# A spectral gated mix on one Trainium2 core: PSUM written in runs of 32 in place of every second place, and the last stores from two queues

## The chip, the cores and the metric

The kernel runs on one core of one Trainium2 chip. The metric is device time in microseconds, the median over runs of the whole program. Before the change it is 128.46 us (three runs, 128.43 to 128.71).

## The reference

Both branches are given the same x; a second x among the inputs is not used. What is computed, cut to what matters:

```python
# x: (1, 2048, 1024) bf16; w_r, w_i: (2048, 513) each, for A and for B; gate_w: (1024)
def branch(x, w_r, w_i):
    X = rfft2(x.astype(float32), axes=(-2, -1))
    return irfft2(X * (w_r + 1j * w_i), s=(2048, 1024)).astype(bfloat16)

g = sigmoid((x * gate_w).sum(-1, keepdims=True))     # one number a row
out = g * branch(x, A_w_r, A_w_i) + (1 - g) * branch(x, B_w_r, B_w_i)
```

So there is one forward transform of x, two products with weights, and two backward transforms that are mixed row by row.

## The kernel before, in words

The transforms are done as matmuls with constant matrices that are loaded from HBM. A helper, `Prog`, records every operation with what it reads and writes; each engine then runs its own operations in the order in which they were recorded, with semaphore waits only where another engine's result or buffer is needed. An engine never goes past an operation that waits, and neither does the queue of DMA issues of an engine (SP's and POOL's here; ACT issues one load at the very start).

In order of time:

- Stage 1 (`stage1`, L380): x is loaded, folded on DVE (L345), and multiplied on PE with the first factor of the transform over the 2048 rows. The results go to the tile FT on ACT (L389) and DVE (L387).
- Steps 0 to 15 (`step`): `stage4(i)`, `swap(i)`, `stage2(i + 2)`, and `products`. `stage2` does the transform over the 1024 columns. For odd columns it issues 8 matmuls of 128 columns (L443), for even ones 8 matmuls of 64 columns (L452); together they fill two banks of PSUM, eight blocks of 128 columns. ACT copies these 1024 columns to XF as bf16 (L458); it reads them in the order in which the next stage wants them. The banks are 0 and 1 for all steps but `stage2(1)` (4 and 5) and `stage2` of 9, 11, 13 and 15 (6 and 7). `stage4(i)` does the rest of the transform over the rows, 4 wide matmuls (L473) on the copy, and ACT evicts them (L477). `swap(i)` issues two DMAs that exchange partitions (from POOL's queue in steps 0 to 7, from SP's later). DVE multiplies the result and its exchanged twin by the weights (`product`, L490), in an order written out by hand (`ORDER`). Weights are loaded through SP's queue until about 48 us. In steps 0 to 5, PE also computes the spectrum of the gate (`gate_spectrum`, L502), two times 8 small matmuls a step.
- The first factor of the backward transform over the rows (`group`, L594): 32 groups of 16 matmuls, evicted by ACT (L604) and DVE (L602). Groups 0 to 15 need the first half of the products, 16 to 31 the second. Small pieces of work lie between them (`zsum` L541, `col0` L568, `rbgen` L581).
- Stages 6 and 7, for each of 16 row blocks r: `stage6` (L725) does the second factor and mixes the branches with the gate, and ACT evicts (L735); `stage7` (L750) does the backward transform over the columns. ACT copies one half (L757); DVE forms sums and differences (L797) and POOL the last ones (L802). In blocks 5, 8 and 12 (`HALF`) and in 14 and 15 DVE does the last ones itself (L761). Then the block is stored, 256 KB, from SP's queue (L290 is the line of every DMA issue); block 15 in two stores of 128 KB each.

SP waits for all stores at the end (L835).

The order of the 256 columns within a block of constants for the odd columns, `F2`, and the places in PSUM of odd and even columns:

```python
F2 += [F[0], F[1]]                                              # odd columns
o = ps((b0 + t % 2) * 512 + cs * 256 + 64, [(64, 2), (1, 64)])             # L443: two runs of 64
o = ps((b0 + t % 2) * 512 + cs * 256 + v, [(193 - 2 * v, 2), (2, 32)])     # L452: two times 32 places, 2 apart
dst, src = sl(XF, CSo(i), [(1, 1024)]), ps(b0 * 512, [(128, 8), (1, 64), (64, 2)])   # L458
```

The pairs in an access pattern are (step, count), the outermost first. A place of PSUM is one float32.

Of the kernel before, what the change touches and what calls it, by code (L numbers as in the profile page):

```python
# [25 lines left out]
def make_consts():  # L26
# [27 lines left out]
    F2 = []  # L54
    for cmb, par in ((0, 0), (1, 1), (2, 1), (3, 0)):
        l = 2 * (np.r_[0:64, 128:192, 64:128, 192:256] if par else np.r_[0:64, 129:193, 64:128, 193:256, 128])[None, :] + par
        th = pi2 * l * (dd + 0.5) / 1024
        F = (np.cos(th) if cmb < 2 else np.sin(th)).reshape(2, 128, 256)
        if par:
            F2 += [F[0], F[1]]  # L60
        else:
            F = F[0].reshape(128, 2, 2, 32, 2)
            e = [np.stack([F[:, :, 0, :, w], F[:, :, 1, :, 1 - w]], axis=2).reshape(128, 128) for w in range(2)]
            F2 += e if cmb == 0 else e[::-1]
# [45 lines left out]
    l2, sl_, f = row % 2, (row // 2) % 32, row // 64  # L110
# [15 lines left out]
    for pi in range(2):  # L126
        for h in range(2):
# [5 lines left out]
            a = pi2 * l * (d + 0.5) / 1024  # L133
# [101 lines left out]
def bass_gated_mix__spectral_gfnet__spectral_gfnet__prompt_kernel(nc, A_x, A_w_r, A_w_i, B_x, B_w_r, B_w_i, gate_w, out):  # L235
# [29 lines left out]
    def sl(t, off, dims, p0=0, np_=128, pstep=1):  # L265
        n = t.shape[1]
        return AP(t, p0 * n + off, [[n * pstep, np_]] + [list(x) for x in dims])

    def ps(col, dims):
        return AP(PS, col, [[4096, 128]] + [list(x) for x in dims])  # L270
# [18 lines left out]
    def dma(eng, name, dst, src, **kw):  # L289
        return P.add(eng, lambda e: e.dma_start(dst, src), dma=name, **kw)  # L290
# [143 lines left out]
    def stage2(i, css=(0, 1), ab=(0, 1)):  # L434
        hf, p = divmod(i, 8)
        b0 = 4 if i == 1 else 6 if i in (9, 11, 13, 15) else 0
        if 0 in ab:
            for cs in css:
                for t in (2 * p, 2 * p + 1):
                    for j in range(2):  # L440
                        o = ps((b0 + t % 2) * 512 + cs * 256 + 64, [(64, 2), (1, 64)])
                        rh = sl(F2, 256 + 512 * cs + 256 * j + hf * 128, [(1, 128)])
                        P.add("pe", lambda e, o=o, cs=cs, j=j, t=t, rh=rh: e.matmul(o, fblock(1 + cs, j, t), rh, start=(j == 0), stop=(j == 1)),  # L443
                              r=[("F1", cs, j), "F2"], w=[bank(b0 + t % 2)])
        if 1 in ab:
            for cs in css:
                for t in (2 * p, 2 * p + 1):
                    for w in range(2):
                        v = 1 - w if cs else w
                        o = ps((b0 + t % 2) * 512 + cs * 256 + v, [(193 - 2 * v, 2), (2, 32)])  # L450
                        rh = sl(F2, 1280 * cs + w * 128 + hf * 64, [(1, 64)])
                        op = P.add("pe", lambda e, o=o, cs=cs, t=t, w=w, rh=rh: e.matmul(o, fblock(3 * cs, w, t), rh, start=True, stop=True),  # L452
                                   r=ekeys(p, cs, w) + ["F2"], w=[bank(b0 + t % 2)])
        if css == (0,) or ab == (0,):
            return
        dst, src = sl(XF, CSo(i), [(1, 1024)]), ps(b0 * 512, [(128, 8), (1, 64), (64, 2)])
        kw = dict(r=[bank(b0), bank(b0 + 1)], w=[("CS", i % 3)], after=last1)
        P.add("act", lambda e: e.activation(dst, src, ACT.Copy), **kw)  # L458
        return op
# [280 lines left out]
    def stage7(r):  # L740
        nonlocal pqc
        full, half = r >= 14, r in HALF
        b0 = 2 * (r - 14) if r >= 14 else 4 + 2 * (r % 2)
        oo = OUo + (r % NOU) * 1024
        es = sl(WA, EOo + (r % 2) * 1024, [(1, 1024)]).bitcast(f32)

        def mm(col, c0, n, ri, pi, h, k, last):
            lh = sl(WA, Yo + (pi * 4 + ri * 2 + h) * 2048 + r * 128, [(1, 128)])
            rh = sl(FT, DIo + pi * 2048 + (ri * 2 + h) * 256 + c0 * 4096, [(4096, n), (1, 256)])
            P.add("pe", lambda e: e.matmul(ps(col, [(1, n * 256)]), lh, rh, start=(k == 0), stop=(k == last)),  # L750
                  r=[("Y", r), "DI"] + ["DJ"] * (full or half), w=[bank(col // 512)])

        def ods(s, k, n):
            return sl(WA, oo + 1023 * s + 512 * (1 - 2 * s) * k, [(512 * (1 - 2 * s), n), (1 - 2 * s, 256)])

        def even(c0, n):
            P.add("act", lambda e: e.activation(es[:, :n], ps((b0 + 1) * 512 + c0, [(1, n)]), ACT.Copy), r=[bank(b0 + 1)], w=[("EO", r % 2)], after=[last5])  # L757

        def finals(k0, n, bk, t, o, keys):
            for s, op in enumerate((ALU.add, ALU.subtract)):  # L760
                P.add("dve", lambda e, s=s, op=op: e.tensor_tensor(  # L761
                    out=ods(s, k0, n), in0=ps(bk * 512, [(256, n), (1, 256)]),
                    in1=sl(t, o + 512 * k0, [(1, 512 * n)]).bitcast(f32).rearrange("p (a b) -> p a b", a=n), op=op),
                    r=keys + [bank(bk)], w=[("OU", r % NOU, s, k) for k in range(k0, k0 + n)], after=[last5])

        if full:
            for k in range(4):
                mm((b0 + 1) * 512, 0, 2, 1, k // 2, k % 2, k, 3)
            even(0, 512)
            for k0, n, bk in ((0, 2, b0),) if r == 14 else ((0, 1, b0), (1, 1, 4)):  # L770
                for k in range(4):
                    mm(bk * 512, k0, n, 0, k // 2, k % 2, k, 3)
                finals(k0, n, bk, WA, EOo + (r % 2) * 1024, [("EO", r % 2)])
        elif half:
            for e_ in range(2):
                for k in range(2):
                    mm((b0 + 1) * 512 + e_ * 256, 0, 1, 1, k, k ^ e_, k, 1)
            even(256, 256)
            for k in range(4):
                mm(b0 * 512, 0, 2, 0, k // 2, k % 2, k, 3)  # L780
            to = 4096 + (r % 2) * 1024
            for s, op in enumerate((ALU.add, ALU.subtract)):
                P.add("dve", lambda e, s=s, op=op: e.tensor_tensor(out=sl(MM, to + s * 512, [(1, 512)]).bitcast(f32),
                                                                   in0=ps((b0 + 1) * 512, [(1, 256)]), in1=es[:, :256], op=op),
                      r=[("EO", r % 2), bank(b0 + 1)], w=[("T", r % 2, s), ("GM", 1, 0), ("GM", 1, 1)])
            finals(0, 2, b0, MM, to, [("T", r % 2, 0), ("T", r % 2, 1)])
        else:
            for e_ in range(2):
                for ri in range(2):
                    for k in range(2):  # L790
                        mm((b0 + e_) * 512 + ri * 256, 0, 1, ri, k, k ^ e_, k, 1)
            even(0, 512)
            pk = pqc % NPQ
            pqc += 1
            pq = PQo + pk * 2048
            for s, op in enumerate((ALU.add, ALU.subtract)):
                P.add("dve", lambda e, s=s, op=op: e.tensor_tensor(out=sl(WA, pq + s * 1024, [(1, 1024)]).bitcast(f32), in0=ps(b0 * 512, [(1, 512)]),  # L797
                                                                   in1=es, op=op),
                      r=[("EO", r % 2), bank(b0)], w=[("PQ", pk, s)], after=[last5])
            pv = sl(WA, pq, [(1, 2048)]).bitcast(f32).rearrange("p (a b c) -> p a b c", a=2, b=2)  # L800
            for s, op in enumerate((ALU.add, ALU.subtract)):
                P.add("pool", lambda e, s=s, op=op: e.tensor_tensor(out=ods(s, 0, 2), in0=pv[:, :, 0, :], in1=pv[:, :, 1, :], op=op),  # L802
                      r=[("PQ", pk, 0), ("PQ", pk, 1)], w=[("OU", r % NOU, s, k) for k in range(2)])
        ou = lambda ks: [("OU", r % NOU, s, k) for s in range(2) for k in ks]
        if r < 15:
            return [dma("sp", f"o{r}", outv[:, r, :], sl(WA, oo, [(1, 1024)]), r=ou((0, 1)))]
        both = lambda a: a.rearrange("p (a b) -> p a b", b=256)[:, ::3, :]
        return [dma("sp", "o15a", both(outv[:, r, :]), sl(WA, oo, [(768, 2), (1, 256)]), r=ou((0,))),
                dma("sp", "o15b", outv[:, r, 256:768], sl(WA, oo + 256, [(1, 512)]), r=ou((1,)))]

    outs = []
    stage6(0)
    stage6(1)
    for r in range(16):
        if 0 < r < 14:
            stage6(r + 2)
        outs += stage7(r)
        if r == 0:
            stage6(2)

    with nc.Block() as block:
        sems = {}
# [59 lines left out]
```

## Time and profile before

| | us |
|---|---|
| median of three runs | 128.46 |
| the profiled execution | 128.5 |
| its span, first to last instruction | 126.7 |
| outside the span | 1.8 |

| engine | busy us | share of the span |
|---|---|---|
| DVE | 101.6 | 80% |
| ACT | 98.8 | 78% |
| POOL | 43.0 | 34% |

The granted TensorE clock is 0.99 of full speed. In 40 slices of 3.2 us each, the rows of PE and of the DMA engines are (9 is 90% or more):

```
PE   0398899799999999999999999999799999999930
DMA  3999999999999995336995000000000332444247
```

The DMA engines are full until about 48 us with loads at some 360 GB/s, and are then used in part: for exchanges, for the last constants until about 70 us, and for stores from 97 us on. A group's row in the profile reads: line, engine, operation, written and read tiles, shapes, count, busy time, mean ns of one, and idle time before. A matmul's duration is its way through the array; the distance of two starts is what a matmul costs in a row of them.

### The profile page before, as it was taken

The page shows a single profiled execution, that of the slowest core. Times are in us where ns is not written, and L with a number is a line of the kernel's source. Part 1 is how long each engine was busy: PE and PEld are TensorE (multiplying, and loading weights), DVE is VectorE, ACT ScalarE, POOL GpSimd, SP SyncE. Part 2 cuts the span into 40 slices and gives each one's busy share as a digit, 9 for nine tenths or more (in the row PEclk, how much of TensorE's full clock was granted, in tenths as well). Part 3 has the DMA queues.
Part 4 walks back from the last instruction along what each step waited for, and adds up shares of the span by engine and source line. Part 5 has one row for each costly group of instructions (what it writes and reads, how often), then busy time and mean ns, then how long its engine had stood idle before and what let it go on. Part 6 is the DMA issues. An engine that isn't in the chain of part 4 may idle for free.

```text
span 126.7 us, 3710 instructions
## 1 busy us (share of the span) xinstructions
PE 113.5 (90%) x1570; PEld 97.9 (77%) x1570; DVE 101.6 (80%) x157; ACT 98.8 (78%) x118; POOL 43.0 (34%) x53
## 2 busy tenths in 40 slices
PE   0398899799999999999999999999799999999930
PEld 0276787696868877779999999999799989898520
DVE  0478999699594999999999969999844787877970
ACT  4139876598998999999999998779488968786610
POOL 1000000006456923003050000000009999999970
PEclk9999999999999999999999999999999999999996
DMA  3999999999999995336995000000000332444247
GB/s 95 322 393 422 408 330 363 350 351 354 363 359 360 363 375 223 142 142 170 394 386 218 8 0 5 0 5 0 0 5 0 118 135 83 166 161 175 85 175 242
DMA packets 17505, 26.12 MB, mean 206 GB/s; under 512 B 2000, under 2 KB 10960, under 8 KB 17360
## 3 DMA queue, kind: packets, MB, share of 16 engines
q1 hardware_dynamic: 16512, 23.64, 53.2%
q0 software_dynamic: 832, 2.11, 4.5%
q8 instruction: 12, 0.20, 0.7%
q10 hardware_dynamic: 144, 0.13, 0.4%
q14 instruction: 5, 0.04, 0.1%
HBM read 17.48 MB, written 4.19 MB: 171 GB/s over the span
## 4 chain that ended last, share of the span: by engine, by line
PE 77%; DVE 8%; DMA 5%; issue 2%; ACT 2%; SPq 2%; DVEq 0%
PE PS L594 25%; PE PS L750 13%; PE PS L725 11%; PE PS L473 11%; PE PS L452 6%; PE PS L443 5%; DMA WB<-in_A_x_dram 5%; DVE XF L345 5%; PE PS L502 2%; DVE FT L387 2%; SPq L290 2%; PE PS L380 2%; PE PS L541 1%; DVE WA L761 1%; ACT FT L389 1%
## 5 line engine op out<-in xcount | busy, mean ns | idle before, releaser
L802 POOL TENSOR_TENSOR WA<-WA 128x512 bf16<-128x512 f32 x22 | 27.3, 1291 | 29.7 <-DVE WA L797 29.6
L594 PE MATMUL PS<-CL,WB 128*128 128x128 bf16 x256 | 31.9, 226 | 0.0
L594 PE MATMUL PS<-CL,WA 128*128 128x128 bf16 x256 | 31.7, 223 | 0.0
L594 PEld LDWEIGHTS PS<-CL,WB 128*128 128x128 bf16 x256 | 31.3, 145 | 0.5 <-issue 0.4
L594 PEld LDWEIGHTS PS<-CL,WA 128*128 128x128 bf16 x256 | 31.3, 145 | 0.1
L604 ACT ACTIVATE WB<-PS 128x1024 bf16<-128x1024 f32 (+1 forms) x29 | 27.9, 1037 | 2.2 <-PE PS L594 2.2
L380 PE MATMUL PS<-MM,XF 128*128 128x256 bf16 x128 | 16.0, 288 | 6.6 <-DVE XF L345 5.4
L490 DVE TENSOR_TENSOR WA<-MM,WA 128x2048 bf16<-128x2048 bf16 x16 | 19.5, 1237 | 2.2 <-DMA MM<-XF 2.2
L735 ACT ACTIVATE WA<-PS 128x1024 bf16<-128x1024 f32 (+1 forms) x16 | 15.9, 997 | 6.7 <-PE PS L725 6.7
L490 DVE TENSOR_TENSOR WB<-XF,WA 128x2048 bf16<-128x2048 bf16 x16 | 19.6, 1234 | 1.5 <-ACT XF L477 1.5
L380 PEld LDWEIGHTS PS<-MM,XF 128*128 128x128 bf16 x128 | 12.8, 103 | 9.5 <-DVE XF L345 5.3
L797 DVE TENSOR_TENSOR WA<-PS,WA 128x512 f32<-128x512 f32 x22 | 14.2, 686 | 6.7 <-ACT WA L757 4.2
L750 PE MATMUL PS<-FT,WA 128*128 128x256 bf16 (+1 forms) x132 | 19.3, 292 | 0.0
L477 ACT ACTIVATE XF<-PS 128x1024 bf16<-128x1024 f32 x16 | 17.2, 1078 | 1.6 <-PE PS L473 1.6
L458 ACT ACTIVATE XF<-PS 128x1024 bf16<-128x1024 f32 x16 | 16.8, 1058 | 0.9 <-PE PS L452 0.9
L473 PE MATMUL PS<-XF,CK 128*128 128x512 bf16 (+1 forms) x72 | 16.7, 358 | 0.0
L750 PEld LDWEIGHTS PS<-FT,WA 128*128 128x128 bf16 x132 | 12.3, 98 | 3.2
L290 POOL DMA_DIRECT2D MM<-XF x16 | 8.8, 555 | 17.1 <-PE PS L473 12.1
L389 ACT ACTIVATE FT<-PS 128x1024 bf16<-128x1024 f32 x12 | 11.5, 1025 | 3.2 <-PE PS L380 3.2
L443 PEld LDWEIGHTS PS<-F,FT 128*128 128x128 bf16 x128 | 8.0, 98 | 3.8 <-ACT XF L458 2.1
L345 DVE TENSOR_TENSOR XF<-WB 128x512 bf16<-128x512 bf16 (+1 forms) x20 | 6.0, 365 | 6.0 <-DMA WB<-in_A_x_dram 6.0
L443 PE MATMUL PS<-F,FT 128*128 128x128 bf16 x128 | 10.0, 220 | 0.0
(74 smaller groups left out, 143.6 us busy)
## 6 DMA issues: line engine op xcount, KB each, us to landing
out_dram<-WA SPq DMA_DIRECT2D x15, 256.0 KB, 2.0
MM<-XF POOLq DMA_DIRECT2D x16, 128.0 KB, 5.3
MM<-XF SPq DMA_DIRECT2D x16, 128.0 KB, 2.7
FT<-c_U SPq DMA_DIRECT2D x1, 2048.0 KB, 9.8
WB<-in_A_x_dram SPq DMA_DIRECT2D x3, 512.0 KB, 6.0
WA<-in_A_w_r_dram SPq DMA_DIRECT2D x4, 256.5 KB, 6.3
WA<-in_A_w_i_dram SPq DMA_DIRECT2D x4, 256.5 KB, 6.3
WA<-in_B_w_r_dram SPq DMA_DIRECT2D x4, 256.5 KB, 6.3
```

Of the source, the lines that this page charges most:

```text
L380: P.add("pe", lambda e, o=o, lh=lh, rh=rh, s=s: e.matmul(o, lh, rh, start=(s == 0), stop=(s == 1)), r=[("xf", c % 2, q, h, s ^ j), ("M", c ...
L443: P.add("pe", lambda e, o=o, cs=cs, j=j, t=t, rh=rh: e.matmul(o, fblock(1 + cs, j, t), rh, start=(j == 0), stop=(j == 1)), r=[("F1", cs, j ...
L458: P.add("act", lambda e: e.activation(dst, src, ACT.Copy), **kw)
L473: P.add("pe", lambda e, o=o, kind=kind, pm=pm, m=m, rh=rh: e.matmul(o, sl(CK, fbo(kind, pm, m), [(1, 128)]), rh, start=(m == 0), stop=(m = ...
L477: P.add("act", lambda e: e.activation(dst, ps(b0 * 512, [(256, 2), (512, 2), (1, 256)]), ACT.Copy), r=[bank(b0), bank(b0 + 1)], w=[("X", i ...
L490: P.add("dve", lambda e: e.tensor_tensor(out=at(sw), in0=sl(xt, xo, [(0, 2), (128, 8), (1, 128)]), in1=at(1), op=ALU.mult), r=[xk] + [("c2 ...
L594: P.add("pe", lambda e, o=o, l0=l0, ab=ab: e.matmul(o, sl(WT[ab], l0, [(RWS[ab] // 2, 128)]), sl(CL, KIo[ab], [(1, 128)]), start=(ab == 0) ...
L604: P.add("act", lambda e, s=src, d=dst: e.activation(d, s, ACT.Copy), r=b, a=["Z"])
L735: P.add("act", lambda e, s=src, d=dst: e.activation(d, s, ACT.Copy), **kw)
L750: P.add("pe", lambda e: e.matmul(ps(col, [(1, n * 256)]), lh, rh, start=(k == 0), stop=(k == last)), r=[("Y", r), "DI"] + ["DJ"] * (full o ...
L797: P.add("dve", lambda e, s=s, op=op: e.tensor_tensor(out=sl(WA, pq + s * 1024, [(1, 1024)]).bitcast(f32), in0=ps(b0 * 512, [(1, 512)]), in ...
L802: P.add("pool", lambda e, s=s, op=op: e.tensor_tensor(out=ods(s, 0, 2), in0=pv[:, :, 0, :], in1=pv[:, :, 1, :], op=op), r=[("PQ", pk, 0), ...
```

## The change

Two things are changed.

First, where `stage2` writes. Each block of 128 places in PSUM held even columns at even or odd places (every second) of one half and odd columns in 64 places side by side. Now a block is made of four runs of 32 places; even columns take two of them and odd columns the other two. The columns of `F2` for the odd columns are put in another order to fit, and ACT reads four runs of 32 in turn (step 32, four deep) where it read two runs of 64. What ACT writes is the same.

Second, the stores of the last three row blocks. They are recorded after all other work, in the order 14, 15a, 13, 15b, where it was 13, 14, 15a, 15b. 14 and 15b are issued from ACT's queue, 15a and 13 from SP's.

```diff
-            F2 += [F[0], F[1]]
+            F2 += [g.reshape(128, 4, 32, 2).transpose(0, 1, 3, 2).reshape(128, 256) for g in F]
...
-                        o = ps((b0 + t % 2) * 512 + cs * 256 + 64, [(64, 2), (1, 64)])
+                        o = ps((b0 + t % 2) * 512 + cs * 256 + 32, [(96, 2), (64, 2), (1, 32)])
...
-                        o = ps((b0 + t % 2) * 512 + cs * 256 + v, [(193 - 2 * v, 2), (2, 32)])
+                        o = ps((b0 + t % 2) * 512 + cs * 256 + 64 * v, [(224 - 128 * v, 2), (1, 32)])
...
-        dst, src = sl(XF, CSo(i), [(1, 1024)]), ps(b0 * 512, [(128, 8), (1, 64), (64, 2)])
+        dst, src = sl(XF, CSo(i), [(1, 1024)]), ps(b0 * 512, [(128, 8), (1, 32), (32, 4)])
...
+        full2 = lambda a: a.rearrange("p (a b) -> p a b", b=256)[:, ::3, :]
         ou = lambda ks: [("OU", r % NOU, s, k) for s in range(2) for k in ks]
+        store = lambda eng, name, dst, src, ks: lambda: dma(eng, name, dst, src, r=ou(ks))
         if r < 15:
-            return [dma("sp", f"o{r}", outv[:, r, :], sl(WA, oo, [(1, 1024)]), r=ou((0, 1)))]
-        both = lambda a: a.rearrange("p (a b) -> p a b", b=256)[:, ::3, :]
-        return [dma("sp", "o15a", both(outv[:, r, :]), sl(WA, oo, [(768, 2), (1, 256)]), r=ou((0,))),
-                dma("sp", "o15b", outv[:, r, 256:768], sl(WA, oo + 256, [(1, 512)]), r=ou((1,)))]
-
-    outs = []
+            return [store("act" if r == 14 else "sp", f"o{r}", outv[:, r, :], sl(WA, oo, [(1, 1024)]), (0, 1))]
+        return [store("sp", "o15a", full2(outv[:, r, :]), sl(WA, oo, [(768, 2), (1, 256)]), (0,)),
+                store("act", "o15b", outv[:, r, 256:768], sl(WA, oo + 256, [(1, 512)]), (1,))]
+
+    outs, late = [], []
...
-        outs += stage7(r)
+        late += stage7(r)
+        if r < 13:
+            outs.append(late.pop()())
...
+    outs += [late[k]() for k in (1, 2, 0, 3)]
```

## The prediction, made before the changed kernel was run

> **What bounds the kernel now.** I read the page first, then the groups with shapes kept apart, then the chain of waits, and then the timelines of PE, ACT, DVE, POOL and SP around the two places that the diff touches.
>
> ```profile
> PE 113.5 (90%) x1570; PEld 97.9 (77%) x1570; DVE 101.6 (80%) x157; ACT 98.8 (78%) x118; POOL 43.0 (34%) x53
> ```
>
> TensorE is the busiest, but its 90% is a mean over stages with different limits. The groups of the two lines of stage 2, and of one small line that writes PSUM without gaps (L568):
>
> ```profile
> L443 PE MATMUL PS<-F,FT 128*128 128x128 bf16 x128 | 10.0, 220 | 0.0
> L452 PE MATMUL PS<-F,FT 128*128 128x64 bf16 x96 | 7.3, 244 | 0.0
> L568 PE MATMUL PS<-PST,CL 128*128 128x64 bf16 x2 | 0.4, 190 | 0.0
> L568 PE MATMUL PS<-PST,CL 128*128 128x60 bf16 x2 | 0.4, 188 | 0.0
> ```
>
> A matmul at L452 has half the columns of one at L443 and lasts longer. What counts is the pace. The chain of waits (start, us, what) and PE's timeline of L568 give it:
>
> ```profile
> 29.45 0.49 PE PS L443 x8
> 29.95 0.45 PE PS L452 x8
> 30.39 0.38 PE PS L502 x16
> 30.77 0.89 PE PS L473 x4
> ```
>
> ```profile
> 68.25 0.25 PE L568 MATMUL PS<-PST,CL 128*128 128x64 bf16 x4
> 68.36 0.38 PE L568 MATMUL PS<-WA,CL 128*128 128x64 bf16 x2
> ```
>
> L452 goes at 0.45/8 = 56 ns, the pace of L443, which has twice the columns. L568 starts four matmuls (64, 60, 2 and 2 columns) from 68.25 to 68.36, 27 ns each, so 64 columns that lie side by side cost about 28 ns, and 60 columns in two runs of 30 no more. L502 loads new weights every 0.38/16 = 24 ns, so weight loads do not hold L452 at 56. The second place on which L452 writes does.
>
> Is PE the limit there? The timeline of ACT (start, us), once while the gate spectrum still runs, once after it:
>
> ```profile
> 31.69 1.02 ACT L477 ACTIVATE XF<-PS 128x1024 bf16<-128x1024 f32 x1 [0.24 <-PE PS L473]
> 32.62 1.02 ACT L458 ACTIVATE XF<-PS 128x1024 bf16<-128x1024 f32 x1
> ...
> 49.50 1.12 ACT L477 ACTIVATE XF<-PS 128x1024 bf16<-128x1024 f32 x1
> 50.41 1.13 ACT L458 ACTIVATE XF<-PS 128x1024 bf16<-128x1024 f32 x1
> ```
>
> From about 40.4 on ACT has no gap and starts an eviction every 0.90 to 0.92 us: 1.81 to 1.83 a step, against 0.45 + 0.45 + 0.86 = 1.76 of PE. There ACT is the limit. DVE (products, L490) is close behind:
>
> ```profile
> 40.35 1.24 DVE L490 TENSOR_TENSOR WA<-MM,WA 128x2048 bf16<-128x2048 bf16 x1 [1.89 <-DMA MM<-XF]
> ...
> 48.79 1.24 DVE L490 TENSOR_TENSOR WA<-MM,WA 128x2048 bf16<-128x2048 bf16 x1 [0.26 <-DMA MM<-XF]
> ...
> 71.15 1.22 DVE L490 TENSOR_TENSOR WA<-MM,WA 128x2048 bf16<-128x2048 bf16 x1
> ```
>
> After 40.35 it waits once more, for 0.26, and its last product ends at 72.37. PE's group 16 (L594) needs all products and starts at 72.65. From there to 89.2 PE is the limit; after that POOL runs its 22 operations (L802) nearly without a gap from 94.94 to 122.61. The end, in the timelines of POOL and SP:
>
> ```profile
> 97.67 24.94 POOL L802 TENSOR_TENSOR WA<-WA 128x512 bf16<-128x512 f32 x20 [0.21 <-DVE WA L797]
> ```
>
> ```profile
> 122.63 0.33 SPq L290 DMA_DIRECT2D out_dram<-WA  x1
> 123.01 0.43 SPq L290 DMA_DIRECT2D out_dram<-WA  x1
> 123.49 0.99 SPq L290 DMA_DIRECT2D out_dram<-WA  x2
> ```
>
> Row block 13's store goes out at 122.63 when POOL is done; 14, 15a and 15b stand behind it on SP and go at 123.01, 123.49 and 123.98. They land at 124.66, 125.41, 125.86 and 126.22, and the span closes 0.46 after the last.
>
> **Part 1: runs of 32.** 128 matmuls at L452 go from 56 to 28 ns: 128 x 0.028 = 3.6 us of PE, 0.22 a step. L443's 128 columns fall into four runs of 32 where there were two of 64; I take 56 ns for them still, by the runs of 30 at L568. L458 reads PSUM at a step of 32 instead of 64 (four words deep instead of two); L604 reads eight deep at a step of 128 and also shows 1.02 us where ACT is not behind, so I take no cost. F2 has the same bytes in another order. How much of the 3.6 us shortens anything is worked out by stages.
>
> Start (23.8 to 26.3): 16 of the matmuls, 0.45 us of PE. But the last four wait for DVE's fold into VD, which starts at 24.50 after PE has read VD and cannot start before DVE's fold into EO ends at 24.32. So 0.18 there and 4 x 0.028 = 0.11 behind it: 0.3.
>
> Six steps with gate spectrum (to 40.4): stage 2 starts at 29.33, 31.51 and 33.69, 2.18 apart. It refills banks 0 and 1, so it waits for L458; L458 waits for L477, which ACT runs before it; L477 waits for L473. One turn of this covers two steps: stage 2 at 29.33, L473's end, L477 at 31.69, L458 at 32.62 and to 33.64, stage 2 at 33.69. Only one of the two L452 blocks lies on it, since the second (done at 32.58) ends just as ACT comes free. So two steps gain 0.22, one 0.11, six 0.67. PE's own work per step, 2.18 - 0.22 = 1.96, stays under the new 2.07.
>
> Steps after that: ACT's 32 evictions are back to back already, so nothing more is gained; PE, at 1.76 - 0.22 = 1.54 a step, only waits for ACT. It waits already: L473 of step 14 starts at 53.43, 0.06 after its eviction ends. Of 3.6 us of PE, 0.3 + 0.67 = 1.0 arrives, and up to 0.15 more where ACT had a last gap at 40.4: I take 1.1.
>
> Products: the one at 40.35 waits for the swap of step 2, whose data come 0.3 + 2 x 0.11 = 0.5 earlier; the 0.26 at 48.79 goes too, as its swap has 1.0. That makes DVE 0.8 earlier if the swaps land earlier by as much as they are issued. The last product then ends at 71.57 and PE, at 72.65 - 1.1 = 71.55, starts group 16 at 71.63: **1.0 us**. If the swaps land when they did (the queue is full of weights until 48), DVE does not move, and the gain is 72.65 - 72.43 = 0.2. I take 1.0: swaps of successive steps are issued 2.2 us apart and land between 1.4 and 3.5 apart, so they follow their issue more than a fixed time. After group 16 nothing waits for a fixed time, since no load lands after 70.5: the shift is carried to the end.
>
> **Part 2: the stores.** The order on SP becomes 15a, 13; on ACT, 14, 15b. ACT's last eviction (L757) ends at 121.20, so nothing but the stores is queued behind its waits. Block 14's data are ready at 121.23: issued at 121.3. 15a is ready at 122.05 and is issued until 122.53, so 13, behind it on SP and ready at 122.61, goes at 122.63 as before. 15b is ready at 122.71 and goes at 122.77 on ACT. Before, 768 KB were moved from 123.5 to 125.6 (374 GB/s) with a silent queue from 122.45 to 123.5. Block 14's 256 KB now fill that hole, and 15a's 128 KB are mostly through before 13: what comes after 13 is 15b alone, 128 KB or 0.35 us. So the last lands at 124.66 + 0.35 = 125.0, to 125.2 if 15a is still in the way: 1.0 to 1.2, I take **1.1 us**. Bounds: an issue from ACT shows once, at the start (0.36 us to issue 128 KB, 3.8 to landing, while x is loaded). With 3.8 for 15b it lands at 126.6, a loss of 0.35; issued at 122.77 with SP's 2.25 it lands at 125.0, a gain of 1.2. I take the latter, as the early row shared the engines with x.
>
> **Sum.** Profiled execution 128.5 us (span 126.7 and 1.8 outside it), 0.04 over the median of the runs: 128.5 - 1.0 - 1.1 = **126.4**.
>
> **Rivals.** (a) The swaps stay: 128.5 - 0.2 - 1.1 = 127.2. For it: the 1.89 us gap is put to a DMA amid weights, and single packets are late by 2 us. (b) Short runs cost as steps do. By the first rows, two runs of 64 at L443 and runs of 30 at L568 are at full pace, but neither row has four runs. If L452 stayed at 56 and L443 went to 112, a step would have 0.45 more on PE: six steps at half of it, 1.35, and eight in which PE's 2.21 exceeds ACT's 1.81, 3.2; less the stores' 1.1 that is 128.5 + 4.55 - 1.1 = 132.0. It turns the sum from 75 ns per matmul at L443 on: 19 ns more are 0.15 a step, which is 0.46 in six and 0.65 in eight, the 1.1 of the stores. The Trainium skill ("PSUM — Partial Sum Buffer", Specifications) says that PSUM has 8-byte lines and that any access pattern with gaps slows matmuls significantly. By its "any" the change leaves L452 slow; by the rows only the step of two does. (c) L452 stays at 56 and L443 too: the stores alone, 127.4. (d) Both L452 blocks count in every two steps, and the products are not in the way: 0.3 + 6 x 0.22 = 1.6, with 1.2 from the stores: 125.7. (e) Stores from ACT land late and (a) holds: 128.5 - 0.2 + 0.35 = 128.6, no change.
>
> **How the numbers follow.** Forecast 0.58, (a) 0.15, (b) 0.06, (c) 0.08, (d) 0.09, (e) 0.04. 0.2% is 0.26 us, about what a measurement of this kernel can tell from no change. Faster: forecast, (a), (c), (d): 0.90. Same: 0.03 of (e). Slower: (b), and the 0.01 of (e) that ends later still, 0.07. The range leaves out (b) and (e) and covers the bounds of the others: from (d) with 0.3 more, 125.4, to (c) with 0.1 less, 127.5.
>
> **What would show it.** Right: L452's block at 0.22 to 0.25 for 8; L443 unchanged; stage 2 about 2.07 apart at first; ACT back to back at 0.90 from about 39.3; group 16 at about 71.6, right behind the last product; four stores, the last landing about 2.4 us after POOL's end rather than 3.6. Wrong: L452 still near 56 ns, L443 above 60, the product after the swap of step 2 still at 40.35, or a store on ACT that takes over 3 us.

## The result and the profile after

The changed kernel takes 127.09 us (median of four runs; before 128.47 beside it), a ratio of 0.987 with a 95% interval of 0.983 to 0.991: 1.4 us faster by the medians, 1.1 to 2.2 by the interval. The profiled execution took 127.11, its span 125.3 (before 126.7). A few executions run some 6 us longer at a lower granted clock; the ratios, the medians from here on and the rows leave them out, but for rows before 65 us in the profiles of `runs_only` and `more_pe_345678`, whose clock falls after that (0.50 and 0.67 of full speed from 70 to 75 us). Run once more as `both` the changed kernel took 127.18 against 128.66, 0.9871 [0.9847, 0.9896].

The page's engine line, then the groups with shapes kept apart:

```profile
PE 112.7 (90%) x1570; PEld 95.6 (76%) x1570; DVE 101.5 (81%) x157; ACT 98.8 (79%) x118; POOL 44.0 (35%) x53
```

```profile
L443 PE MATMUL PS<-F,FT 128*128 128x128 bf16 x128 | 10.0, 220 | 0.1
L452 PE MATMUL PS<-F,FT 128*128 128x64 bf16 x96 | 4.8, 193 | 0.0
```

PE is still 90% busy, so that line tells nothing of what was won. In the groups L443 is where it was and one matmul at L452 lasts 193 ns in place of 244. The pace stands in the chain of waits (start, us, what), here over two steps of the first stretch:

```profile
28.18 0.92 ACT XF L458
29.11 0.05 issue
29.15 0.62 PE PS L443 x8
29.77 0.23 PE PS L452 x8
30.01 0.38 PE PS L502 x16
30.39 0.89 PE PS L473 x4
31.27 0.51 PE PS L443 x8
31.78 0.23 PE PS L452 x8
32.02 0.38 PE PS L502 x16
32.40 0.89 PE PS L473 x4
33.28 0.02 issue
33.30 0.62 PE PS L443 x8
```

L452 goes at 0.23/8 = 29 ns. Two steps take 33.30 - 29.15 = 4.15 us, where before they took 33.69 - 29.33 = 4.36. PE gave up 2 x 0.22 of work in them and only 0.21 came off the time. Every second L443 block now takes 0.62 instead of 0.51, and ACT's L458 stands ahead of one: PE has begun to wait for the bank.

ACT's timeline, in that stretch, after it, and at its last eviction at L477:

```profile
31.31 1.02 ACT L477 ACTIVATE XF<-PS 128x1024 bf16<-128x1024 f32 x1 [0.20 <-PE PS L473]
32.23 1.02 ACT L458 ACTIVATE XF<-PS 128x1024 bf16<-128x1024 f32 x1
...
46.85 1.10 ACT L477 ACTIVATE XF<-PS 128x1024 bf16<-128x1024 f32 x1
47.76 1.12 ACT L458 ACTIVATE XF<-PS 128x1024 bf16<-128x1024 f32 x1
...
56.88 1.25 ACT L477 ACTIVATE XF<-PS 128x1024 bf16<-128x1024 f32 x1
```

The evictions cost what they did (1.02, and one every 0.91 when back to back), so reading four runs of 32 costs no more than two of 64. The last L477 starts at 56.88 against 57.72. DVE's products:

```profile
39.96 1.27 DVE L490 TENSOR_TENSOR WA<-MM,WA 128x2048 bf16<-128x2048 bf16 x1 [2.06 <-DMA MM<-XF]
...
48.05 1.22 DVE L490 TENSOR_TENSOR WA<-MM,WA 128x2048 bf16<-128x2048 bf16 x1
...
66.01 1.28 DVE L490 TENSOR_TENSOR WA<-MM,WA 128x2048 bf16<-128x2048 bf16 x1 [0.24 <-DMA MM<-XF]
...
70.64 1.22 DVE L490 TENSOR_TENSOR WA<-MM,WA 128x2048 bf16<-128x2048 bf16 x1
```

The product after the swap of step 2 starts at 39.96 (40.35 before), the wait at 48.79 is gone, and a new one of 0.24 has come at 66.01. The last product starts 0.51 earlier. Then POOL and the last four issues, which are blocks 14, 15a, 13 and 15b:

```profile
96.94 24.94 POOL L802 TENSOR_TENSOR WA<-WA 128x512 bf16<-128x512 f32 x20 [0.21 <-DVE WA L797]
```

```profile
120.53 0.38 ACTq L290 DMA_DIRECT2D out_dram<-WA  x1
...
121.35 0.39 SPq L290 DMA_DIRECT2D out_dram<-WA  x1
...
121.90 0.48 SPq L290 DMA_DIRECT2D out_dram<-WA  x1
...
122.02 0.35 ACTq L290 DMA_DIRECT2D out_dram<-WA  x1
```

POOL's run starts at 96.94 (97.67): 0.73 was won by then. It ends at 121.88, the last landing is at 124.79, 2.91 behind it where it was 3.61: another 0.70. Together 1.43, the difference of the spans.

So that profiles can be compared whose stage 1 ended at other times (22.1 to 22.7), the table counts from the first L443 of stage 2. The last columns are from POOL's end to the last landing and, of the 16 DMA engines, to the end of the middle one. Group 17 stands there for group 16, since only the second matmul of group 16 needs the last product: a wait for it lies inside that group, and group 17 shows it.

| kernel | stage 2 of step 8 | last L477 starts | last product ends | group 17 starts | last landing | middle engine |
|---|---|---|---|---|---|---|
| before | 17.84 | 35.32 | 49.97 | 51.23 | 3.61 | 3.48 |
| changed | 16.94 | 34.36 | 49.35 | 50.38 | 2.91 | 2.47 |
| both | 16.94 | 34.36 | 49.46 | 50.48 | 2.79 | 2.40 |
| stores_only | 17.84 | 35.32 | 49.99 | 51.23 | 2.90 | 2.41 |
| runs_only | 16.94 | 34.45 | | | | |
| more_pe_357 | 17.61 | 35.02 | 48.90 | 50.95 | | |
| more_pe_468 | 17.39 | 34.91 | 49.16 | 50.82 | | |
| more_pe_345678 | 17.80 | 35.32 | | | | |
| u5_last | 16.94 | 34.35 | 48.18 | 50.27 | | |
| store12_first | 16.93 | 34.35 | 49.76 | 50.80 | 2.61 | 2.52 |
| combo | 16.94 | 34.36 | 49.53 | 50.55 | 2.60 | 2.54 |

### The profile page after: what moved, and what is told of

Its sections match the earlier page's. It is cut to its first block, busy times and chain, and to the rows that moved or that the text cites. A ratio compares the mean times of both kernels' runs of the same rounds, so it can differ in the third digit from the quotient of the medians.

```text
span 125.3 us, 3710 instructions
## 1 busy us (share of the span) xinstructions
PE 112.7 (90%) x1570; PEld 95.6 (76%) x1570; DVE 101.5 (81%) x157; ACT 98.8 (79%) x118; POOL 44.0 (35%) x53
## 4 chain that ended last, share of the span: by engine, by line
PE 71%; DVE 8%; ACT 7%; DMA 5%; issue 3%; SPq 2%; DVEq 0%
PE PS L594 25%; PE PS L750 13%; PE PS L725 12%; PE PS L473 9%; DMA WB<-in_A_x_dram 5%; DVE XF L345 5%; PE PS L443 4%; ACT XF L458 3%; PE PS L502 2%; PE PS L452 2%; ACT XF L477 2%; DVE FT L387 2%; SPq L290 2%; PE PS L380 2%; PE PS L541 1%
## 5 line engine op out<-in xcount | busy, mean ns | idle before, releaser
L380 PE MATMUL PS<-MM,XF 128*128 128x256 bf16 x128 | 16.9, 299 | 5.8 <-DVE XF L345 5.3
L380 PEld LDWEIGHTS PS<-MM,XF 128*128 128x128 bf16 x128 | 13.4, 107 | 9.0 <-DVE XF L345 5.2
L477 ACT ACTIVATE XF<-PS 128x1024 bf16<-128x1024 f32 x16 | 17.4, 1085 | 0.9 <-PE PS L473 0.6
L458 ACT ACTIVATE XF<-PS 128x1024 bf16<-128x1024 f32 x16 | 16.9, 1062 | 0.6 <-PE PS L452 0.6
L473 PE MATMUL PS<-XF,CK 128*128 128x512 bf16 (+1 forms) x72 | 16.5, 356 | 0.6
L443 PEld LDWEIGHTS PS<-F,FT 128*128 128x128 bf16 x128 | 7.9, 98 | 4.4 <-ACT XF L458 2.8
L443 PE MATMUL PS<-F,FT 128*128 128x128 bf16 x128 | 10.0, 220 | 0.1
```

Source lines behind the costliest of these rows:

```text
L380: P.add("pe", lambda e, o=o, lh=lh, rh=rh, s=s: e.matmul(o, lh, rh, start=(s == 0), stop=(s == 1)), r=[("xf", c % 2, q, h, s ^ j), ("M", c ...
L473: P.add("pe", lambda e, o=o, kind=kind, pm=pm, m=m, rh=rh: e.matmul(o, sl(CK, fbo(kind, pm, m), [(1, 128)]), rh, start=(m == 0), stop=(m = ...
L477: P.add("act", lambda e: e.activation(dst, ps(b0 * 512, [(256, 2), (512, 2), (1, 256)]), ACT.Copy), r=[bank(b0), bank(b0 + 1)], w=[("X", i ...
```

## The experiments

**Each part alone.** `stores_only` is the kernel before with the last two hunks of the diff; `runs_only` is the changed kernel with the old code for the stores; `both` is the changed kernel again.

> Part 1 alone: runs of 32 in PSUM, the stores as before. Theory (both parts count: about 0.7 us from the matmuls, 0.7 us from the stores): 127.7 us, L452 at 29 ns, last product about 0.5 us earlier than before, the last landing 3.6 us after POOL's end. Rival (all of the gain is the stores', since ACT is full in these steps): 128.4 us.

> Part 2 alone: every second place in PSUM as before, the stores in the new order from two queues. Theory: 127.8 us, POOL's end where it was (122.6), the last landing 2.9 us after it instead of 3.6. Rival (all of the gain is the matmuls'): 128.4 us, the last landing 3.6 us after POOL's end. Rival (as predicted, 2.4 us after POOL's end): 127.4 us.

> The changed kernel once more, on the chip and beside the runs of the two kernels with one part each. Theory: 127.1 us, the sum of the two parts' gains. Rival (the parts get in each other's way, so that the sum of both gains is over 0.3 us more than the gain of both): 127.4 us or more.

Beside 128.66: `runs_only` 127.70, 0.9929 [0.9898, 0.9960]; `stores_only` 127.83, 0.9941 [0.9921, 0.9960]; `both` 127.18. By the ratios the parts win 0.91 and 0.76 us, together 1.67, and `both` wins 1.66; by the medians it is 0.96 and 0.83, together 1.79, against 1.48. So each part wins by itself, and they add to within some 0.3 us, which is as far as these runs can tell. The rows agree: `runs_only` has step 8 at 16.94, where the changed kernel has it; `stores_only` is the kernel before up to group 17, within 0.02, and the changed one after POOL.

**What makes a write to PSUM slow.** `pairs` keeps even columns at places that are not side by side, but in runs of two:

```diff
-g.reshape(128, 4, 32, 2).transpose(0, 1, 3, 2)
+g.reshape(128, 4, 16, 2, 2).transpose(0, 1, 2, 4, 3)
-o = ps((b0 + t % 2) * 512 + cs * 256 + 32, [(96, 2), (64, 2), (1, 32)])
+o = ps((b0 + t % 2) * 512 + cs * 256 + 2, [(126, 2), (4, 32), (1, 2)])
-o = ps((b0 + t % 2) * 512 + cs * 256 + 64 * v, [(224 - 128 * v, 2), (1, 32)])
+o = ps((b0 + t % 2) * 512 + cs * 256 + 4 * v, [(134 - 8 * v, 2), (8, 16), (1, 2)])
-ps(b0 * 512, [(128, 8), (1, 32), (32, 4)])
+ps(b0 * 512, [(8, 128), (1, 2), (2, 4)])
```

> The changed kernel with runs of 2 places in PSUM instead of 32, for even and odd columns alike (so L443 and L452 both write 8 bytes, then skip 24). Theory (two places side by side, 8 bytes, are written in one go, so that only the step of two is slow): L452 at 29 ns, L443 at 56 ns, 127.1 us. Rival (every gap costs, or short runs do): L452 at 56 ns and L443 at 112 ns, about 131 us; L452 at 56 and L443 at 56, about 127.8 us.

127.11 against 128.66, 0.9867 [0.9844, 0.9890], the same as `both`. The chain of waits of `pairs`:

```profile
29.29 0.62 PE PS L443 x8
29.91 0.23 PE PS L452 x8
```

Runs of two cost nothing, for 64 columns or 128. `pairs_odd` shifts them by one place for one half of the matmuls, `+ (cs == 0)` in both `o`, while ACT reads from where it did.

> The kernel with runs of 2 places, but for the first half of the columns (cs = 0, half of the matmuls at L443 and L452) all runs are written one place further on, so that each begins at an odd place; the eviction still reads the old places, so that half of its numbers are not the reference's. Theory (PSUM is written in lines of two places, 8 bytes, that begin at even places; a matmul pays for each line it touches): the matmuls with cs = 0 at 56 ns at L452 and 112 ns at L443, those with cs = 1 at 29 and 56 ns. Rival (two neighbours go together wherever they begin): 29 and 56 ns in both halves.

It was run once, 129.17 us. PE's timeline of `pairs_odd` after the gate spectrum:

```profile
46.55 0.82 PE L443 MATMUL PS<-F,FT 128*128 128x128 bf16 x8
47.21 0.50 PE L452 MATMUL PS<-F,FT 128*128 128x64 bf16 x8
47.55 1.03 PE L473 MATMUL PS<-XF,CK 128*128 128x512 bf16 x4
```

From start to start the 8 matmuls of L443 take 0.66 (0.45 where nothing is shifted) and those of L452 0.34 (0.23). By single records, the shifted halves go at 108 ns (L443) and 56 ns (L452), the others at 56 and 29. The number of runs is the same in both halves, so it is not the gaps that cost: a pair at an even place is one write, and a pair that straddles two such places costs as much as two single ones. That is also the price of every second place. The Trainium skill ("PSUM — Partial Sum Buffer", Specifications) says that PSUM has 8-byte lines, which is two of these places, and this agrees; its remark that any non-contiguous pattern slows matmuls significantly is borne out for every second place (56 ns in place of 29), but not for runs of two at even places.

**Why half of the saving in the first six steps.** The prediction put one L452 block in two on the path. To test it, PE was given back about 0.22 us in some steps, four matmuls of 128 columns into bank 7, whose results nothing reads, ahead of the even columns; one run each for odd steps, even steps, and all six.

```diff
+        if i in (3, 5, 7):          # (4, 6, 8); (3, 4, 5, 6, 7, 8)
+            for q in range(4):
+                P.add("pe", matmul(ps(7 * 512, [(1, 128)]), fblock(1, 0, 2 * p), sl(F2, 256 + hf * 128, [(1, 128)])), ...)
```

> The changed kernel with four more matmuls of 128 columns (0.22 us of PE, into a bank nobody reads, so the result is the same) between L443 and L452 of stage 2 for steps 3, 5 and 7: as much PE time put back as the change took from these three. Theory (one turn of evictions covers two steps, and these three blocks lie on it): stage 2 of step 8 starts 0.6 to 0.7 later than in the changed kernel, ACT's last L477 too. Rival (PE time is free here, since ACT is full): under 0.1 later. Total by the theory 127.6 to 127.9, by the rival 127.2.

> The same four matmuls in stage 2 for steps 4, 6 and 8 instead. Theory (these blocks end while ACT is still busy, with 0.19 to spare): stage 2 of step 8 starts at most 0.1 later than in the changed kernel, total 127.2. Rival (all PE time counts alike): 0.45 later there and 0.67 after step 8, total as with steps 3, 5 and 7.

Medians 127.58 and 127.44 against 128.91: 0.9911 [0.9883, 0.9939] and 0.9894 [0.9861, 0.9928]. The odd steps cost what the prediction's chain says: step 8 is 17.61 - 16.94 = 0.67 late, three times 0.22, and two steps take 4.37. In the chain of waits of `more_pe_357` (L447 are the added matmuls, L456, L477 and L506 what was L452, L473 and L502):

```profile
29.07 0.62 PE PS L443 x8
29.69 0.22 PE PS L447 x4
29.91 0.23 PE PS L456 x8
...
31.41 0.51 PE PS L443 x8
31.92 0.23 PE PS L456 x8
...
33.44 0.62 PE PS L443 x8
34.06 0.22 PE PS L447 x4
```

But the even steps, which I had expected to cost next to nothing (0.1 at most at step 8), cost 0.45 there and 0.55 at the last L477. One chain through every second block is not the whole of it. ACT's timeline of `more_pe_468` (L481 is L477, L462 is L458):

```profile
31.34 1.02 ACT L481 ACTIVATE XF<-PS 128x1024 bf16<-128x1024 f32 x1 [0.20 <-PE PS L477]
32.35 1.02 ACT L462 ACTIVATE XF<-PS 128x1024 bf16<-128x1024 f32 x1
33.57 1.02 ACT L481 ACTIVATE XF<-PS 128x1024 bf16<-128x1024 f32 x1 [0.20 <-PE PS L477]
```

L462 starts 1.01 after L481, not 0.92 as in the changed kernel, and its stage 2 is at 35.56 where the one two steps earlier was at 31.19: 4.37 again. It is not PE itself that is full there: its blocks make 0.51 + 0.23 + 0.38 + 0.89 = 2.01 a step, twice that and 0.22 is 4.24. So there are two interlaced turns of L452, L473, L477, L458 and stage 2 two steps on, and the later of the two decides. Mended like this, the theory has a consequence of its own: slowing both must cost as much as slowing one, until PE's own work is longer than either.

> The changed kernel with the four extra matmuls (0.22 us of PE) in stage 2 of all steps from 3 to 8. Theory, mended after the runs with three of them each (two turns of evictions are laced into each other, each covers two steps and holds every second block, and the later of the two decides): no more than with steps 3, 5 and 7 alone: from the first stage 2 to that of step 8 17.5 to 17.8 us (changed kernel 16.94), to ACT's last L477 34.9 to 35.2 (34.36). Rival (all PE time counts): 16.94 + 5 x 0.22 = 18.06 and 35.7. Total by the theory as with three, by the rival 0.6 more.

Step 8 is at 17.80 (the mended theory said 17.5 to 17.8, the sum of both 18.06) and the last L477 at 35.32, just above the theory's 34.9 to 35.2 and under the sum's 35.7; two steps take 4.47 where the sum would be 4.60. That is above 4.37, and the chain shows why: 0.51 + 0.22 + 0.23 + 0.38 + 0.89 = 2.23 of PE a step with no wait between, a third limit. The kernel before stood at both at once: its chain was PE without a gap as well, at 2.18. The median is 128.28 against 128.68, 0.9979 [0.9950, 1.0009]. By the ratios that is 0.9 above `more_pe_357`, where the theory said no more and its rival 0.6. Part of it is in the table: the last L477 is back where the kernel before has it (35.32), so that of the change only the stores were left to win, and `stores_only` had 0.9941 [0.9921, 0.9960]. What costs the rest stays open. The rows speak for two turns, the total does not.

**The wait at 66.** What the product waits for is the swap of step 14, which lands at 65.98, behind a 2 MB load of a constant that lands at 65.30 (`U5`, issued at L635 on SP's queue, as the swap is). The wait is not a product of the change alone: `stores_only`, with the old places in PSUM, has it too. Its first and its last wait for a swap in DVE's timeline:

```profile
38.69 1.24 DVE L490 TENSOR_TENSOR WA<-MM,WA 128x2048 bf16<-128x2048 bf16 x1 [0.34 <-DMA MM<-XF]
...
66.45 1.24 DVE L490 TENSOR_TENSOR WA<-MM,WA 128x2048 bf16<-128x2048 bf16 x1 [0.72 <-DMA MM<-XF]
```

`u5_last` issues that load behind the last swap:

```diff
-        if i == 13:
+        if i == 15:
```

> The changed kernel with the load of 2 MB (U5) issued after the swaps of steps 14 and 15 instead of before them. Theory (the swap of step 14 is held by this load until 66.0, so the last product ends 0.1 after PE is ready for group 16): no wait of the product at 66.0, the last product 0.2 to 0.4 earlier, group 16 without a stall, total 0.1 less: 127.1. Rival (the swap lands late anyway): still a wait near 66, total 127.2. Bound the other way: the load lands after 69 and keeps L581 waiting past 72.9, slower than 127.3.

127.20 against 128.91, 0.9894 [0.9851, 0.9936]. DVE's timeline of `u5_last`, where the last product is the third line:

```profile
65.10 1.23 DVE L490 TENSOR_TENSOR WA<-MM,WA 128x2048 bf16<-128x2048 bf16 x1
...
67.38 1.23 DVE L490 TENSOR_TENSOR WA<-MM,WA 128x2048 bf16<-128x2048 bf16 x1
...
69.67 1.23 DVE L490 TENSOR_TENSOR WA<-MM,WA 128x2048 bf16<-128x2048 bf16 x1
```

There is no wait, the swap of step 14 lands at 59.3 rather than 66.0, and the products end 1.17 earlier than in the changed kernel (48.18 against 49.35), where 0.2 to 0.4 was expected. The load itself lands at 69.25, before L581 first runs at 71.95, so the bound the other way was not reached. Not all of the 1.17 is this edit's: the swap of step 2 landed at 38.61 here and at 39.94 in the changed kernel, and `combo` below, which has the same edit, has its last product no earlier (49.53). Group 17 moves by 0.11 alone: by then PE is the later of the two: it has worked without a gap since 54 us, and ACT's last L477 ahead of it has not moved. So the wait at 66 delayed DVE by more than it delayed the end. In the total, 0.1 can't be told apart.

**Which store is last.** In the changed kernel block 12's store, ready by 118.4, stands on SP behind block 11's, which waits for POOL until 119.4. `store12_first` puts all late stores in the order in which they are ready: 12, 11, 14, 15a, 13, 15b.

```diff
-        if r < 13:
+        if r < 11:
...
-    outs += [late[k]() for k in (1, 2, 0, 3)]
+    outs += [late[k]() for k in (1, 0, 3, 4, 2, 5)]
```

> The changed kernel with block 12's store ahead of block 11's on SP (12 is ready 1.5 us before 11). Theory (the last stores are late because the DMA engines, above all the slowest, still have the stores of 11, 12, 14 and 15a to move): the last landing 2.4 to 2.5 us after POOL's end instead of 2.9, total 126.8. Rival (13 and 15b, issued 0.1 apart, hinder each other, whatever came before): 2.9 us as now, total 127.2.

126.78 against 128.91, 0.9855 [0.9812, 0.9898]; the interval overlaps that of `both`. The DMA engines' share in 40 slices, for the changed kernel from 119 to 125.3 us and for `store12_first` from 119 to 125.6:

```profile
DMA  0000004899999999998995699999400000000000
```

```profile
DMA  1399940002699930079993698799999500000000
```

In the changed kernel the transfers stand in one heap from 120 on; with block 12 out early they are spread, with holes ahead of the last. The last landing is 2.61 behind POOL's end in place of 2.91, between the 2.4 to 2.5 of the theory and the 2.9 of its rival. The other profiles agree: 2.60 and 2.61 where block 12 is first (`combo` and `combo_order`, below), 2.72 to 2.92 where block 11 is and the new order follows. The middle engine did not gain (2.52 against 2.47); the slowest one came to within 0.1 of it.

The trace also shows something that was not tested. Amid block 11's store one packet of another queue is moved, an 8 KB load of instructions, here in the changed kernel's DMA queues from 120 to 121 us:

```profile
q14 instruction: 1, 0.01, 4.1%
```

That is 0.66 us of one of the 16 engines, starting at 120.13. Of block 11's store 15 engines end by 121.43 and the last at 122.04, 0.61 later. The same pair is 0.70 and 0.75 before, 0.55 and 0.47 in `both`, 0.63 and 0.61 in `store12_first`; there the last engine has caught up by block 14's store (123.25, the one before it 123.21), while in the changed kernel it is still 0.35 behind in block 13's. So the slowest engine is probably the one that carried this load. Which engine that was is not recorded, and no run moved the load.

**The best version.** `combo` is the changed kernel with both edits. `combo_order` also exchanges two neighbours in `ORDER`, the products `(2, 1)` and `(4, 0)`.

> The changed kernel with both: block 12's store ahead of block 11's, and the 2 MB load (U5) after the swaps of steps 14 and 15. Theory (the two add: 0.1 at group 16, 0.2 to 0.3 behind POOL's end): 0.3 to 0.4 us under the changed kernel, ratio to before 0.984 to 0.985. Rival (PE at group 16 and the last stores are bounded by something else): ratio 0.987 as for the changed kernel.

> As before this one, and the first product of step 4 ahead of the second of step 2 in DVE's order, which fills the gap in which DVE waits for the swap of step 2. Theory (after the load is moved DVE is 1.1 ahead of PE at group 16, so that more lead is worth nothing): the last product 0.5 to 1.1 earlier, total as without. Rival (DVE still limits somewhere between 40 and 72): 0.3 us less.

`combo` took 126.63 against 128.62, 0.9837 [0.9810, 0.9865], the fastest of all; its interval overlaps that of `both`, and in its profile group 17 is no earlier, so the tail's 0.2 to 0.3 is all that can be pointed to. DVE's timeline of `combo` has a wait, for the swap of step 6, that the changed kernel's profile has not:

```profile
48.51 1.31 DVE L490 TENSOR_TENSOR WA<-MM,WA 128x2048 bf16<-128x2048 bf16 x1 [1.36 <-DMA MM<-XF]
```

`combo_order` took 127.02, 0.9876 [0.9846, 0.9906]: no gain, as its theory said. Its profile is no verdict on the order: the granted clock was 0.64 from 27 to 30 us (1.00 in `combo`), the first 8 matmuls at L473 took 1.77 in place of 0.94, and step 8 is 1.39 late, from a place far ahead of the exchanged products.

## Why the prediction was right, point by point

**L452 at half.** 56 to 29 ns, forecast 28. `pairs_odd` shows what the rows of before could not: it is the place of the pairs, not the step, that matters. L443 stayed at 56 and L458 at 1.02, as costed. The rivals in which L452 stays slow or L443 doubles fell; that L443 can go at 108 ns, with pairs at odd places, was seen.

**The start.** 0.3 forecast, 0.29 by the stage 2 starts.

**The six steps.** 0.67 forecast, 0.61 measured; two steps at 2 x 2.07 as worked out. The number was right, the reason only half: not one chain but two, of which the later decides, and the rival that both blocks count in every two steps, which would make them 3.9, fell with the 4.15 itself. With the last gap, ACT's end at L477 came 0.96 earlier for 1.1 forecast.

**The products.** In this pair of profiles the swap of step 2 landed 0.4 earlier, as its issue did, and the wait at 48.79 went. That it followed its issue is not shown by this: in `stores_only`, with the old places in PSUM, the same swap landed at 38.66, 1.67 ahead of the kernel before, so a swap's landing scatters by more than the change moves it. The middle of the 16 engines moved by 0.31 (38.60 to 38.29) for an issue 0.39 earlier; the scatter is in the slowest one. The step that was missed: "After 40.35 it waits once more" was a statement about one profile. With DVE earlier, the swap of step 14 was late, and the last product came 0.5 earlier, not 0.8. Counted from stage 2, it ends at 49.97 and 49.99 in the two profiles with the old places and at 48.18 to 49.76 in all with the new ones but `pairs_odd`: DVE does come earlier, by an amount that scatters, and that the term came out as near as it did was in part luck. As `u5_last` shows, the wait at 66 cost group 17 only 0.1. The shift at group 17 was 0.85 where 1.0 was forecast, from the same start of stage 2; stage 1 itself ended 0.12 later in this profile, which leaves the 0.73 at POOL.

**The stores.** All four issues went out as forecast, and the middle DMA engine ended 2.47 behind POOL, for 2.4 forecast. The step that failed is the one that takes the 16 engines as one and adds bytes over bandwidth ("128 KB or 0.35 us"): the last landing is that of the slowest engine, at 124.79, 0.44 behind the middle one. "What comes after 13 is 15b alone" did not hold either in this profile: the last to land was block 13's own store, while 15b was through by 124.4; in `both` and `stores_only` it was 15b, 0.2 behind 13. What mattered in all of them was what stood ahead of 13. Block 12's store was still in the heap (its middle engine ended at 121.99, its slowest at 123.32), and `store12_first`, which takes it out, has the engines within 0.1 of each other. Those 0.44 are about the difference between the 1.1 forecast and the 0.70 measured. The stores from ACT took 3.0 (256 KB) and 2.4 us (128 KB) to land, so the one early issue, 3.8 for 128 KB, was no measure of them.

In all, 1.43 for 2.1: the two terms were each some 0.3 to 0.4 too large, the first by the wait for a swap and by stage 1, the second by the slowest engine. The total by itself would have spoken for a rival: 127.1 is nearer to (a), 127.2, and to (c), 127.4, than to the forecast's 126.4. The rows decide against both, with L452 at 29 ns and group 17 0.85 earlier where (a) has 0.2.

## What to carry to other kernels

Before counting what a faster instruction brings, find in each stage what its engine waits for next: here a PE saving counted by two thirds at the start (0.29 of 0.45 us), by half where two turns over shared banks stood close behind, and not at all where ACT was full. Write PSUM so that two neighbouring float32 at an even place go together; more than that was not needed here. On a queue that waits for its data, put the stores in the order in which they become ready, and judge the end by the slowest of the DMA engines, not by bytes over bandwidth.

## What the runs showed of the hardware that was not expected

Runs of two at even places go at full pace (29 ns for 64 columns, 56 for 128), at odd places at half (56 and 108).

The 16 DMA engines do not end together. The 2 MB load of `U5` was issued at 55.48 before, at 54.66 in the changed kernel and at 54.47 in `both`; the middle engine ended at 64.74, 63.13 and 62.93, the slowest at 65.30 in all three. That the last figure is three times the same is no rule: it is 65.09 in `pairs`, 65.76 in `stores_only` and 65.97 in `store12_first`. What holds the slowest one back in this load was not tried.
